# Attention and two MLP layers on one core: the first MLP phase in 256-token tiles, two output blocks to a PSUM bank, and an emission order by due times

## The chip, the core and the metric

One NeuronCore of one Trainium2 chip runs the whole program in one launch. The metric is the device time in microseconds. Engines are named as the profile names them: PE (matmul) and PEld (its weight loads), DVE (vector), ACT (scalar activations), POOL, and SP, which here only issues DMAs.

## What is computed

The reference, cut to what matters (B=4, H=8, S=576, D=64; 2304 tokens of 512 values, d_ff=2048):

```python
scores = q @ k.T / sqrt(64)              # per batch and head, 576 x 576
mask = (rel >= 0) & (rel < 64)           # each query sees itself and the 63 keys before it
attn = exp(scores - rowmax); attn = attn / (rowsum + 1e-9)
x = (attn @ v).transpose(0, 2, 1, 3).reshape(2304, 512)
h = x @ moe_w_in;   x = maximum(0.01 * h, h) @ moe_w_out
h = x @ moe2_w_in;  out = (h * cos(h)) @ moe2_w_out
```

## The kernel before

**Attention** runs in 18 *steps* of 128 tokens, all 8 heads at once, as two halves (the even and the odd heads, `hd` 0 and 1). A step is a chain over four engines. PE makes the scores `qk` into two PSUM buffers (`a_scores`). DVE scales and masks them into `S` and takes the row maxima, half by half (`a_mask`). ACT exponentiates with the row sums (`a_exp`, four instructions a half). DVE inverts the sums (`a_recip`), POOL scales the rows (`a_norm`, L309), PE transposes (`pt`, L317), ACT copies the transposed block to SBUF (`PT`), PE multiplies by the values (`pv`, L329), ACT writes the rounded result `XH` and DVE the remainder `XL`. So `XH` + `XL` hold the layer's input in two parts, step by step.

**The MLPs** multiply in split precision: every product is three matmuls (high by high, high by low, low by high). Each layer's 16 blocks of 128 hidden units are taken in four *phases* of G=4 blocks, so there are eight phases in all. Within a phase the tokens go in tiles, and one tile with one block is a *unit*. A unit `i` has 12 matmuls `h` (L421 to L423: input by w_in, four chunks of the model dimension), then on ACT and DVE the activation `ca`, its rounded part `gh` and its remainder `gl` (L431, L436), then 12 matmuls `y` (L505, called `o` below: `emit_O`), which add into four output accumulators over the four units of a tile. After a tile's last unit ACT copies the four accumulators to `YFa` or `YFb` (`evac`). The first phase's tiles hold 256, 256, 512, 512, 512 and 256 tokens, so it has units 0 to 23, and unit 24 begins the second phase.

**The weights** arrive as 64-bit words and are rebuilt on the core, one matrix block (a *weight unit* `u`) at a time: ACT takes the words apart (`wa`, `wf`), DVE sets the bits (L200, L201, L205), POOL multiplies and adds (`wf`, L210; `wa`, L214), ACT rounds to `wh`, POOL makes the remainder `wl` (L226). The first phase needs eight weight units; those of the second need SBUF that attention gives back when its last step is over (`a_close`), so only three of them can be begun before that.

**The order of the work.** From the start to the end of the first phase, and two units further, a greedy planner written in Python (`ListSchedule`) sets the order in which instructions are emitted, with a table of assumed durations and of buffers. Each engine then runs its own instructions strictly in that order. The planner takes, of all the steps that could go next, the one with the earliest start plus a fixed `bias` by kind. Buffers are counted in it: `S` 4, `PT` 2, PSUM banks `y` 4, `h` 2 and `a` 2 (the last for scores, transposes and `pv`). From unit 26 on, a plain loop emits H of unit `i`, its activation, and O of unit `i-2`.

The line that picks the engine for a step that could go to several:

```python
rank = t + us + (DVE_SPARED if engine == "dve" and len(ways) > 1 else 0.0)
```

Of the kernel before, what the change touches and what calls it, by code (L numbers as in the profile page):

```python
# [31 lines left out]
TILES_FIRST = (256, 256, 512, 512, 512, 256)  # L32
# [3 lines left out]
B_MLP = 0.0  # L36
B_W = 0.25
B_W2 = 1.0
B_ATT = 0.0
DVE_SPARED = 2.0  # L40
# [3 lines left out]
class ListSchedule:  # L44
# [11 lines left out]
    def add(self, name, ways, after=(), take=(), give=(), bias=0.0):  # L56
        assert name not in self.ops
        self.ops[name] = (ways, tuple(after), tuple(take), tuple(give), bias)

    def ready(self, name):  # L60
        ways, after, take, give, bias = self.ops[name]
# [11 lines left out]
        for engine, us, fn in ways:  # L73
            t = max(bufs, self.free.get(engine, 0.0))
            for a in after:
                t0, e0 = self.done[a]
                t = max(t, t0 + (0.02 if e0 == engine else 0.35 if e0 == "pe" else 0.2))
            rank = t + us + (DVE_SPARED if engine == "dve" and len(ways) > 1 else 0.0)
            if best is None or rank < best[4]:
                best = (t, engine, us, fn, rank)  # L80
        return best

    def run(self):
        waiting = list(self.ops)
        while waiting:
            best = None
            for name in waiting:
                r = self.ready(name)
                if r is not None and (best is None or r[0] + self.ops[name][4] < best[0]):
                    best = (r[0] + self.ops[name][4], name, r)  # L90
            assert best is not None, waiting[:40]
            _, name, (t, engine, us, fn, _) = best
# [13 lines left out]
def attention_two_mlps(ctx, tc, q, k, v, w_in1, w_out1, w_in2, w_out2, out, seq):  # L106
# [18 lines left out]
    ps_y = ctx.enter_context(tc.tile_pool(name="ps_y", bufs=4, space=bass.MemoryType.PSUM))  # L125
# [216 lines left out]
    def a_close():  # L342
# [4 lines left out]
        late["ps_y2"] = ctx.enter_context(tc.tile_pool(name="ps_y2", bufs=2, space=bass.MemoryType.PSUM))  # L347
# [130 lines left out]
    def emit_O(i, chunks=None):  # L478
# [4 lines left out]
        first, last = w["first"], w["last"]  # L483
# [4 lines left out]
        for d in range(nacc) if chunks is None else chunks:  # L488
            if first:
                pool = ps_y  # L490
                if "ps_y2" in late:
                    pool = late["ps_y2"] if ycount[0] % 6 >= 4 else ps_y
                    ycount[0] += 1
                ys.append(pool.tile([P, 512], F32, tag="y", name=f"y{i}_{d}"))
            if l == 0:
                y = ys[d][:, :n]
                prods = [(wh[:, 1, d, :], gh[:, :n]), (wh[:, 1, d, :], gl[:, :n]), (wl[:, 1, d, :], gh[:, :n])]
            else:
                y = ys[d]
# [4 lines left out]
            for x, (a, b) in enumerate(prods):  # L504
                mm(y, a, b, start=first and x == 0, stop=last and x == 2)  # L505
            if last:
                e_todo.append((w, d, y))
        if d == nacc - 1:
# [34 lines left out]
    for kind, m in enumerate(masks):  # L543
# [18 lines left out]
        dict(a=2, y=4, h=2, S=4, PT=2, ca=2, g=2, wa=3, wf=2, we=1),  # L562
# [7 lines left out]

    def add_w_dma(x):
# [4 lines left out]
            bias=B_W if x < 2 * G else B_W2,  # L576
# [183 lines left out]
```

## Time and profile before

| | |
|---|---|
| median of 3 runs | 931.75 us (928.1 to 936.08) |
| the profiled execution | 934.54 us, its span 932.7 us |
| mean granted PE clock | 0.977 |
| PE busy | 883.8 us (95%), 5136 matmuls |
| DVE, ACT, POOL busy | 589.1 us (63%), 485.9 us (52%), 306.6 us (33%) |
| DMA | 60.11 MB, mean 64 GB/s, 231 GB/s in the first 23 us |

The profile shows one execution. Its span runs from the first to the last instruction, and the execution's own time is 1.84 us above it. Times in its rows are microseconds from the span's start. In a timeline row stand the start, the duration, the engine and line, what is written and read, and how often; in brackets the idle time before it and what ended it. A matmul's duration is a model that overlaps the next one's, so how fast PE goes is read from the starts.

### The profile page before, as it was taken

The page shows a single profiled execution, that of the slowest core. Times are in us where ns is not written, and L with a number is a line of the kernel's source. Part 1 is how long each engine was busy: PE and PEld are TensorE (multiplying, and loading weights), DVE is VectorE, ACT ScalarE, POOL GpSimd, SP SyncE. Part 2 cuts the span into 40 slices and gives each one's busy share as a digit, 9 for nine tenths or more (in the row PEclk, how much of TensorE's full clock was granted, in tenths as well). Part 3 has the DMA queues.
Part 4 walks back from the last instruction along what each step waited for, and adds up shares of the span by engine and source line. Part 5 has one row for each costly group of instructions (what it writes and reads, how often), then busy time and mean ns, then how long its engine had stood idle before and what let it go on. Part 6 is the DMA issues. An engine that isn't in the chain of part 4 may idle for free.

```text
span 932.7 us, 13579 instructions
## 1 busy us (share of the span) xinstructions
PE 883.8 (95%) x5136; PEld 737.5 (79%) x5136; DVE 589.1 (63%) x935; ACT 485.9 (52%) x1079; POOL 306.6 (33%) x267
## 2 busy tenths in 40 slices
PE   5778979799899999999999999999999999999998
PEld 4667767579688888888888888888887888788886
DVE  5787635355665545555576577776787777876555
ACT  5667555555533333332445467667556556554443
POOL 4772311114733213322367443332332233320000
PEclk9889899899999999999999999999999999999999
DMA  7644433301212101110111111110111011001111
GB/s 231 197 151 147 147 103 109 116 4 46 91 47 67 40 29 46 46 46 23 45 46 50 42 45 46 46 46 22 50 64 41 28 45 46 24 1 46 46 45 69
DMA packets 29089, 60.11 MB, mean 64 GB/s; under 512 B 2464, under 2 KB 11680, under 8 KB 29024
## 3 DMA queue, kind: packets, MB, share of 16 engines
q1 hardware_dynamic: 29024, 59.25, 19.3%
q8 instruction: 40, 0.66, 0.3%
q14 instruction: 25, 0.20, 0.1%
HBM read 54.53 MB, written 4.72 MB: 64 GB/s over the span
## 4 chain that ended last, share of the span: by engine, by line
PE 85%; DVE 7%; ACT 4%; issue 2%; POOL 2%; DMA 1%; SPq 0%; DVEq 0%; ACTq 0%; POOLq 0%
PE y L505 38%; PE h L421 14%; PE h L422 13%; PE h L423 13%; PE pv L329 3%; PE qk L279 2%; PE pt L317 2%; DVE wa L201 1%; POOL S L309 1%; ACT S L297 1%; ACT PT L153 1%; DVE wa L200 1%; DVE we L205 1%; DVE S L287 1%; DVE sm L292 1%
## 5 line engine op out<-in xcount | busy, mean ns | idle before, releaser
L421 PE MATMUL h<-XH,wh 128*128 128x512 f32 (+1 forms) x656 | 243.2, 371 | 6.0 <-DVE ca L443 3.2
L422 PE MATMUL h<-XL,wh 128*128 128x512 f32 (+1 forms) x656 | 240.8, 367 | 0.0
L423 PE MATMUL h<-XH,wl 128*128 128x512 f32 (+1 forms) x656 | 240.6, 367 | 0.1
L226 POOL TENSOR_TENSOR wl<-wa,wh 128x512 fp32r<-128x512 f32 x64 | 85.8, 1343 | 217.6 <-ACT wh L153 216.2
L421 PEld LDWEIGHTS h<-XH,wh 128*128 128x128 f32 x656 | 125.7, 192 | 30.2 <-DVE ca L443 4.5
L436 DVE TENSOR_TENSOR gl<-ca,gh 128x512 fp32r<-128x512 f32 (+1 forms) x164 | 139.2, 848 | 10.3 <-ACT gh L153 10.3
L423 PEld LDWEIGHTS h<-XH,wl 128*128 128x128 f32 x656 | 125.3, 191 | 20.5 <-POOL wl L226 0.3
L422 PEld LDWEIGHTS h<-XL,wh 128*128 128x128 f32 x656 | 125.7, 192 | 19.9
L431 DVE TENSOR_TENSOR ca<-h,ca 128x512 f32<-128x512 f32 (+1 forms) x84 | 51.5, 613 | 132.5 <-ACT ca L153 132.3
L153 ACT ACTIVATE gh<-ca 128x512 fp32r<-128x512 f32 (+1 forms) x164 | 94.4, 576 | 78.0 <-PE y L505 60.2
L210 POOL TENSOR_TENSOR wf<-wf,we 128x512 bf16<-128x512 bf16 x63 | 73.3, 1163 | 179.2 <-DVE we L205 169.7
L505 PE MATMUL y<-gh,wh 128*128 128x512 f32 (+1 forms) x336 | 123.9, 369 | 0.0
L505 PE MATMUL y<-gh,wl 128*128 128x512 f32 (+1 forms) x336 | 121.5, 362 | 1.8 <-POOL wl L226 1.8
L505 PE MATMUL y<-gl,wh 128*128 128x512 f32 (+1 forms) x336 | 121.4, 361 | 0.5 <-DVE gl L436 0.5
L505 PE MATMUL y<-wh,gh 128*128 128x512 f32 x288 | 112.4, 390 | 0.3 <-ACT gh L153 0.3
L505 PE MATMUL y<-wl,gh 128*128 128x512 f32 x288 | 112.2, 390 | 0.0
L505 PE MATMUL y<-wh,gl 128*128 128x512 f32 x288 | 112.2, 389 | 0.0
L461 DVE SCALAR_TENSOR_TENSOR cb<-ca,h 128x512 f32<-128x512 int32 (+1 forms) x80 | 50.7, 633 | 84.2 <-ACT ca L459 84.2
L153 ACT ACTIVATE ca<-h 128x512 f32<-128x512 f32 (+1 forms) x83 | 44.6, 538 | 112.8 <-PE h L423 106.4
L468 ACT ACTIVATE cb<-ca 128x512 f32<-128x512 f32 (+1 forms) x80 | 47.2, 590 | 79.5 <-DVE ca L462 79.5
L459 ACT ACTIVATE ca<-h 128x512 int32<-128x512 f32 (+1 forms) x80 | 44.2, 552 | 80.0 <-PE h L423 78.9
L214 POOL TENSOR_TENSOR wa<-wa,wf 128x512 f32<-128x512 f32 x63 | 79.4, 1260 | 4.7
(59 smaller groups left out, 1265.1 us busy)
## 6 DMA issues: line engine op xcount, KB each, us to landing
st<-in_moe_w_in_dram SPq DMA_DIRECT2D x32, 512.0 KB, 3.4
st<-in_moe_w_out_dram SPq DMA_DIRECT2D x32, 512.0 KB, 3.4
v<-in_v_dram SPq DMA_DIRECT2D x35, 256.0 KB, 2.9
kT<-in_k_dram SPq DMA_DIRECT2D x17, 384.0 KB, 3.8
qT<-in_q_dram SPq DMA_DIRECT2D x18, 256.0 KB, 3.9
out_dram<-YFa SPq DMA_DIRECT2D x12, 256.0 KB, 2.2
out_dram<-YFb SPq DMA_DIRECT2D x6, 256.0 KB, 2.1
kT<-in_k_dram SPq DMA_DIRECT2D x1, 256.0 KB, 3.3
```

Of the source, the lines that this page charges most:

```text
L153: nc.scalar.activation(out=out_, in_=in_, func=AF.Copy, scale=scale)
L210: engines[engine].tensor_tensor(out=f, in0=f, in1=e, op=ALU.mult)
L214: engines[engine].tensor_tensor(out=a, in0=a, in1=f, op=ALU.add)
L226: engines[engine].tensor_tensor(out=wl, in0=mid.pop(u)[0], in1=wh.bitcast(F32), op=ALU.subtract)
L421: mm(h[:, :n], wh[:, 0, kk, :], xh, start=kk == 0, stop=False)
L422: mm(h[:, :n], wh[:, 0, kk, :], xl, start=False, stop=False)
L423: mm(h[:, :n], wl[:, 0, kk, :], xh, start=False, stop=kk == KD - 1)
L431: nc.vector.tensor_tensor(out=ca[i], in0=hps.pop(i)[:, :work[i]["n"]], in1=ca[i], op=ALU.max)
L436: nc.vector.tensor_tensor(out=gl[:, :n], in0=ca.pop(i), in1=gh[:, :n].bitcast(F32), op=ALU.subtract)
L461: nc.vector.scalar_tensor_tensor(out=b, in0=kk, scalar=-PI2_A, in1=h, op0=ALU.mult, op1=ALU.add)
L468: nc.scalar.activation(out=b, in_=a, func=AF.Sin, scale=0.5)
L505: mm(y, a, b, start=first and x == 0, stop=last and x == 2)
```

## The change

It has three parts, all in the planned stretch (the plain loop behind it is the same but for which pool a PSUM bank comes from).

First, the first phase goes in nine tiles of 256 tokens, so it has units 0 to 35, and unit 36 begins the second phase. Its accumulators are *packed*: two output blocks of 256 columns share one PSUM bank, so a tile takes two banks where it took four, and one copy takes two blocks out.

Second, the buffers are dealt out anew: `y` 2 banks, `a` 4 banks, `S` 6, `PT` 3. Only step 0 uses the `y` banks for its scores (`LEAD`, before: steps 0 and 1).

Third, the planner picks differently. Of all steps that could start within 0.05 us of the earliest, it takes the one with the earliest *due* time: tile `t` is due at 18 `t`, attention step `i` at 9 `i` - 30, the first eight weight units from -22 on, the next at 30 and every 8 us after. The assumed durations are new, and DVE may take POOL's part of the first eight weight units at a smaller handicap (0.3 in place of 2.0).

```diff
-TILES_FIRST = (256, 256, 512, 512, 512, 256)
+TILES_FIRST = (256,) * 9
...
-DVE_SPARED = 2.0
+SAME = dict(pe=0.0, dve=0.12, act=0.12, pool=0.05, dma=0.0, none=0.0)
+AT_ONCE = 0.05
+TILE_US, STEP_AHEAD = 18.0, 30.0
+W_AHEAD, LATE_FROM, LATE_US = 22.0, 30.0, 8.0
+SPARED_FIRST, SPARED = 0.3, 2.0
...
-            rank = t + us + (DVE_SPARED if engine == "dve" and len(ways) > 1 else 0.0)
+            rank = t + us + (spared if engine == "dve" and len(ways) > 1 else 0.0)
...
-                if r is not None and (best is None or r[0] + self.ops[name][4] < best[0]):
-                    best = (r[0] + self.ops[name][4], name, r)
+            now = min(r[0] for _, r in ready) + AT_ONCE
+            name, (t, engine, us, fn, _) = min(
+                (x for x in ready if x[1][0] <= now), key=lambda x: (self.ops[x[0]][4], x[1][0])
+            )
...
-    ps_y = ctx.enter_context(tc.tile_pool(name="ps_y", bufs=4, space=bass.MemoryType.PSUM))
+    ps_y = ctx.enter_context(tc.tile_pool(name="ps_y", bufs=2, space=bass.MemoryType.PSUM))
-    sp = act_es.enter_context(tc.tile_pool(name="sp", bufs=4))
-    ptp = act_es.enter_context(tc.tile_pool(name="ptp", bufs=2))
+    sp = act_es.enter_context(tc.tile_pool(name="sp", bufs=6))
+    ptp = act_es.enter_context(tc.tile_pool(name="ptp", bufs=3))
-    ps_a = act_es.enter_context(tc.tile_pool(name="ps_a", bufs=2, space=bass.MemoryType.PSUM))
+    ps_a = act_es.enter_context(tc.tile_pool(name="ps_a", bufs=4, space=bass.MemoryType.PSUM))
...
+            if packed:
+                y = ys[d // 2][:, d % 2 * n:(d % 2 + 1) * n]
...
+                mm(y, a, b, start=first and x == 0 and not (packed and d % 2), stop=last and x == 2,
+                   skip_group_check=packed)
-            if last:
+            if last and not packed:
                 e_todo.append((w, d, y))
+            elif last and d % 2:
+                e_todo.append((w, d - 1, ys[d // 2]))
...
-        op("wm", ways(lambda e: w_mult(u, e), pool=1.11, dve=0.36), [f"wb{u}"], [], [("we", f"wb{u}")])
+        op("wm", ways(lambda e: w_mult(u, e), pool=1.24, dve=0.42), [f"wb{u}"], [], [("we", f"wb{u}")])
...
+    def s_due(i):
+        return TILE_US / 2 * i - STEP_AHEAD
...
-    LEAD = TILES_FIRST[0] // P
+    LEAD = 1
```

The order on each engine moves with this. Two places follow; the figure behind a name's letters is the step, the unit or the weight unit, and a trailing figure only numbers the buffer.

On DVE, before, around the first unit's activation `ca0` (the bits of weight units 4 and 6 stand beside it, steps 2 and 3 are the scores):

```order
L200 TENSOR_SCALAR wa4_360<-wa4_360 128x512
L201 SCALAR_TENSOR_TENSOR wa4_360<-st4_324,wa4_360 128x512
L205 TENSOR_SCALAR we4_387<-wa4_360 128x512
L287 SCALAR_TENSOR_TENSOR S2_0_365<-qk2_0_364,m2_112 128x512
L292 TENSOR_REDUCE sm2_401<-S2_0_365 128x4
L287 SCALAR_TENSOR_TENSOR S2_1_367<-qk2_1_366,m2_112 128x512
L292 TENSOR_REDUCE sm2_401<-S2_1_367 128x4
L431 TENSOR_TENSOR ca0_420<-h0_395,ca0_420 128x256
L157 TENSOR_SCALAR wf6_458<-st6_362 128x512
L200 TENSOR_SCALAR wa6_409<-wa6_409 128x512
L201 SCALAR_TENSOR_TENSOR wa6_409<-st6_362,wa6_409 128x512
L205 TENSOR_SCALAR we6_460<-wa6_409 128x512
```

On DVE, with the change, around the same `ca0` (`wf5`, `wa5`, `wf7` and `wa7` written from themselves are the product and the sum that POOL made before; their line numbers are one less than before's):

```order
L209 TENSOR_TENSOR wf5_492<-wf5_492,we5_525 128x512
L213 TENSOR_TENSOR wa5_456<-wa5_456,wf5_492 128x512
L199 TENSOR_SCALAR wa7_546<-wa7_546 128x512
L200 SCALAR_TENSOR_TENSOR wa7_546<-st7_497,wa7_546 128x512
L204 TENSOR_SCALAR we7_582<-wa7_546 128x512
L337 TENSOR_TENSOR XL_80<-pv2_553,XH_79 128x4x128
L209 TENSOR_TENSOR wf7_575<-wf7_575,we7_582 128x512
L430 TENSOR_TENSOR ca0_573<-h0_516,ca0_573 128x256
L213 TENSOR_TENSOR wa7_546<-wa7_546,wf7_575 128x512
L435 TENSOR_TENSOR gl0_640<-ca0_573,gh0_639 128x256
L430 TENSOR_TENSOR ca1_612<-h1_536,ca1_612 128x256
L286 SCALAR_TENSOR_TENSOR S4_0_591<-qk4_0_590,m1_111 128x512
```

Before, `ca0` stands behind the bits of three weight units; with the change it stands behind the bits of all eight, and behind eleven products, sums and remainders of them that were POOL's, and `gl0`, on which the first `y` matmul waits, stands just behind it.

On PE, before, where step 10's transposes stand (the rows ahead of them are the end of the scores of step 11 and unit 11's second half of `y`):

```order
L279 MATMUL qk11_0_1540<-kT11_1308,qT11_1310 64x128
L279 MATMUL qk11_1_1542<-kT11_1308,qT11_1310 64x128
L505 MATMUL y8_2_1385<-gh11_1507,wh3_557 128x512
L505 MATMUL y8_2_1385<-gl11_1508,wh3_557 128x512
L505 MATMUL y8_2_1385<-gh11_1507,wl3_558 128x512
L505 MATMUL y8_3_1420<-gh11_1507,wh3_557 128x512
L505 MATMUL y8_3_1420<-gl11_1508,wh3_557 128x512
L505 MATMUL y8_3_1420<-gh11_1507,wl3_558 128x512
L317 MATMUL pt10_0_1589<-ident_109,S10_0_1484 128x128 x4
L317 MATMUL pt10_1_1599<-ident_109,S10_1_1486 128x128 x4
L329 MATMUL pv10_1611<-PT10_0_1604,v10_1417 64x64
```

On PE, with the change, at the same transposes (step 10's scores end 74 rows ahead of this piece, step 11's 57):

```order
L420 MATMUL h15_1649<-XH_79,wh3_439 128x256
L421 MATMUL h15_1649<-XL_80,wh3_439 128x256
L422 MATMUL h15_1649<-XH_79,wl3_440 128x256
L316 MATMUL pt10_0_1663<-ident_109,S10_0_1491 128x128 x4
L420 MATMUL h15_1649<-XH_79,wh3_439 128x256
L421 MATMUL h15_1649<-XL_80,wh3_439 128x256
L422 MATMUL h15_1649<-XH_79,wl3_440 128x256
L420 MATMUL h15_1649<-XH_79,wh3_439 128x256
L421 MATMUL h15_1649<-XL_80,wh3_439 128x256
L422 MATMUL h15_1649<-XH_79,wl3_440 128x256
L316 MATMUL pt10_1_1680<-ident_109,S10_1_1493 128x128 x4
L420 MATMUL h16_1685<-XH_79,wh0_293 128x256
```

Before, both transposes of step 10 and its `pv` stand back to back behind the tile's last `y`; now `h` matmuls of the next units stand ahead of each transpose, and `pv10` follows 28 rows further on.

More of the change, by code (lines that the diff above doesn't have):

```diff
@@ L54, in __init__, with add @@
         self.given = {p: {} for p in pools}
-    def add(self, name, ways, after=(), take=(), give=(), bias=0.0):
+    def add(self, name, ways, after=(), take=(), give=(), due=0.0, spared=0.0):
         assert name not in self.ops
-        self.ops[name] = (ways, tuple(after), tuple(take), tuple(give), bias)
+        self.ops[name] = (ways, tuple(after), tuple(take), tuple(give), due, spared)
     def ready(self, name):
-        ways, after, take, give, bias = self.ops[name]
+        ways, after, take, give, due, spared = self.ops[name]
         bufs = 0.0
@@ L85, in run @@
         while waiting:
-            best = None
-            for name in waiting:
-                r = self.ready(name)
-                if r is not None and (best is None or r[0] + self.ops[name][4] < best[0]):
-                    best = (r[0] + self.ops[name][4], name, r)
-            assert best is not None, waiting[:40]
-            _, name, (t, engine, us, fn, _) = best
+            ready = [(name, r) for name in waiting if (r := self.ready(name)) is not None]
+            assert ready, waiting[:40]
+            now = min(r[0] for _, r in ready) + AT_ONCE
+            name, (t, engine, us, fn, _) = min(
+                (x for x in ready if x[1][0] <= now), key=lambda x: (self.ops[x[0]][4], x[1][0])
+            )
             waiting.remove(name)
@@ L346, in a_close @@
         late["tb"] = ctx.enter_context(tc.tile_pool(name="tb", bufs=2))
[L347 removed]
+        late["ps_y2"] = ctx.enter_context(tc.tile_pool(name="ps_y2", bufs=4, space=bass.MemoryType.PSUM))
         YF[1] = late["yb"].tile([P, (T - T_SPLIT) // P, KD, P], F32, name="YFb")
@@ L482, in emit_O @@
         gh, gl = g_hl[i]
-        first, last = w["first"], w["last"]
+        first, last, packed = w["first"], w["last"], w["packed"]
         nacc = KD if l == 0 else n // P
@@ L488, in emit_O @@
         for d in range(nacc) if chunks is None else chunks:
-            if first:
+            if first and not (packed and d % 2):
                 pool = ps_y
-                if "ps_y2" in late:
-                    pool = late["ps_y2"] if ycount[0] % 6 >= 4 else ps_y
+                if not packed:
+                    pool = ps_y if ycount[0] % 6 < 2 else late["ps_y2"]
                     ycount[0] += 1
                 ys.append(pool.tile([P, 512], F32, tag="y", name=f"y{i}_{d}"))
+            if packed:
+                y = ys[d // 2][:, d % 2 * n:(d % 2 + 1) * n]
+            else:
+                y = ys[d][:, :n] if l == 0 else ys[d]
             if l == 0:
-                y = ys[d][:, :n]
                 prods = [(wh[:, 1, d, :], gh[:, :n]), (wh[:, 1, d, :], gl[:, :n]), (wl[:, 1, d, :], gh[:, :n])]
             else:
-                y = ys[d]
                 sl = slice(d * P, (d + 1) * P)
@@ L665, in add_unit @@
             ls.add(
-                f"o{i}_{d}", ways(lambda e, d=d: emit_O(i, [d]), pe=0.648 * f), after,
-                ["y"] if w["first"] else [], [("g", f"gh{i}")] if d == KD - 1 else [], bias=B_MLP,
+                f"o{i}_{d}", ways(lambda e, d=d: emit_O(i, [d]), pe=0.04 + 0.64 * f), after,
+                ["y"] if w["first"] and d % 2 == 0 else [], [("g", f"gh{i}")] if d == KD - 1 else [], due=u_due(i),
             )
-            if w["last"]:
+            if w["last"] and d % 2:
                 after = [f"o{i}_{d}"]
-                if d:
-                    after.append(f"ev{i}_{d - 1}")
+                if d > 1:
+                    after.append(f"ev{i}_{d - 2}")
                 elif i >= G:
```

72 lines of the change are left out of this document (38 added, 34 removed).

## Prediction

> **What bounds the kernel now.** I read the page first: PE is busy in nearly every slice, and the slices where it is not lie at the left.
>
> ```profile
> PE   5778979799899999999999999999999999999998
> ```
>
> So I cut the span at events of the program. PE's timeline gives them: the first `h`, the first `y` of unit 0, the first `h` of the second phase (unit 24, the first of 512 columns behind 256).
>
> ```profile
> 26.87 0.58 PE L421 MATMUL h<-XH,wh 128*128 128x256 f32 x1
> ...
> 52.63 0.28 PE L505 MATMUL y<-gh,wh 128*128 128x256 f32 x1
> 52.75 0.28 PE L505 MATMUL y<-gl,wh 128*128 128x256 f32 x1
> ...
> 225.26 0.40 PE L421 MATMUL h<-XH,wh 128*128 128x512 f32 x1
> ```
>
> The table by stages (the cuts between are the first `h` of the tiles of 512):
>
> ```profile
> core 0: us, PE busy (x) PEld busy (x) DVE busy (x) ACT busy (x) POOL busy (x), PEclk, DMA share, GB/s
> ...
> 26.90:52.60 25.70, 19.41 (x207) 16.69 (x205) 19.54 (x32) 17.75 (x55) 16.91 (x15) 0.87 0.54 170
> 52.60:97.00 44.40, 35.69 (x423) 31.61 (x421) 32.26 (x57) 29.68 (x101) 22.60 (x19) 0.87 0.47 159
> 97.00:141.60 44.60, 39.15 (x387) 30.48 (x384) 22.64 (x39) 26.09 (x88) 10.92 (x10) 0.94 0.38 123
> 141.60:187.20 45.60, 40.55 (x388) 31.49 (x385) 21.18 (x36) 25.97 (x88) 8.60 (x8) 0.89 0.35 108
> 187.20:225.30 38.10, 38.10 (x284) 32.29 (x282) 18.75 (x33) 21.11 (x61) 10.86 (x9) 0.95 0.05 15
> 225.30:256.50 31.20, 26.72 (x123) 21.69 (x122) 19.60 (x26) 17.60 (x34) 21.10 (x16) 0.95 0.26 85
> ```
>
> Between 52.6 and 225.3 no engine is full: DVE and ACT run at 50 to 75%, and a busy PE is not PE at its peak. How much of these 172.6 us PE needs comes from starts of its rows:
>
> ```profile
> 102.12 1.10 PE L279 MATMUL qk<-kT,qT 64*64 64x128 f32 x32
> 103.15 0.50 PE L421 MATMUL h<-XH,wh 128*128 128x512 f32 x1
> ...
> 107.41 0.60 PE L317 MATMUL pt<-ident,S 128*128 128x128 f32 x4
> 107.76 0.47 PE L505 MATMUL y<-gh,wh 128*128 128x512 f32 x1
> ...
> 116.78 1.08 PE pv L329 x32
> ...
> 253.87 2.74 PE y L505 x12
> ```
>
> A matmul of 512 columns takes 2.74/12 = 0.228 us, one of 256 takes 52.75 - 52.63 = 0.12. A step's scores take 1.03 to 1.10 (I use 1.10), a half's transposes 0.35, with the changeover 0.4, the values 1.08. PE's order before has, from the first `y` to unit 24, 204 matmuls of 256 columns (24.5 us), 288 of 512 (65.7), 13 score groups (14.3), 28 halves of transposes (11.2) and 14 of values (15.1): 130.8 us. So 41.8 us are lost here. The waits name 19.2 of them for this stretch, of which these rows are 14.3:
>
> ```profile
> PE pt L317 <- POOL S L309: 10.6, 9, 3.7
> PE pv L329 <- ACT PT L153: 3.7, 7, 1.1
> ```
>
> Most of the rest is the granted clock: 0.13, 0.06, 0.11 and 0.05 of the four stages from 52.6 on are 5.8 + 2.7 + 5.0 + 1.9 = 15.4 us. **The bound of the first phase is thus the attention chain where PE has too little beside it**, and the half clock that follows such waits.
>
> **The change part by part. Length of the chain, and what lies beside it.** Three steps show how long the chain is from the end of the scores to the first transpose, where PE waited for it:
>
> ```profile
> 26.09 0.86 PE L279 MATMUL qk<-kT,qT 64*64 64x128 f32 x10
> ...
> 38.41 2.29 PE L317 MATMUL pt<-ident,S 128*128 128x128 f32 x8 [4.86 <-POOL S L309]
> ...
> 50.07 1.10 PE L279 MATMUL qk<-kT,qT 64*64 64x128 f32 x30 [1.09 <-DVE XL L338]
> ...
> 60.62 0.55 PE L317 MATMUL pt<-ident,S 128*128 128x128 f32 x3 [3.73 <-POOL S L309]
> ...
> 120.09 1.10 PE L279 MATMUL qk<-kT,qT 64*64 64x128 f32 x32
> ...
> 129.64 0.66 PE L317 MATMUL pt<-ident,S 128*128 128x128 f32 x4 [1.51 <-POOL S L309]
> ```
>
> 38.41 - 26.95 = 11.5 us (step 2, among the weights), 60.62 - 51.17 = 9.45 (step 4), 129.64 - 121.19 = 8.45 (step 10, in the quiet middle). Beside it, PE's order before holds 3.25 to 9.3 us of other work (steps 11 and 15: 3.25; 10 and 14: 6.6). The new order, counted with the same prices, holds for steps 4 to 17: 10.5, 10.9, 8.4, 12.1, 9.1, 9.0, 8.0, 14.9, 8.7, 9.0, 8.4, 9.9, 7.2, 7.3 us. What a chain lacks of cover is PE's wait. With a chain of 8.45 these steps lack 2.9 us in all, with 9.45 they lack 9.8, with 11.5 they lack 32. ACT and DVE have the same work per token as before and less time for it (26.09 us of ACT for 512 tokens in the third row of the table), so their queues are fuller than in the quiet middle; I take 9.45, and 5 us for values, remainders and `gl` (values alone 3.7 before, in the waits): **15 us lost, ends 5 and 37**. The lower end leaves 2 of those 5 us; the upper is 32 and 5. I charge no half clock on top: all covers but a few exceed the wait, so PE should not stand long. If it still falls as before, up to 15 us come back; that is in the upper half of the range.
>
> **PE's work.** With the change, from unit 0's first `y` to unit 36, which begins the second phase, PE has 807 matmuls of 256 columns (96.8 us), 13 score groups (14.3), 28 halves of transposes (11.2) and 15 of values (16.2): 138.5 us. It is more than 130.8 since 27 matmuls of `h` and step 3's values less have gone before the first `y`, and since two matmuls of 256 take 0.240 us where one of 512 takes 0.228: 288 times 0.012 are 3.5 us of cost, which this sum holds.
>
> **The start.** The first `y` needs `gl0` and all of DVE's work ahead of it. The same view by shapes, DVE from 0 to 225 us:
>
> ```profile
> L292 DVE TENSOR_REDUCE sm<-S 128x4 f32<-128x512 f32 x36 | 24.7, 686 | 1.2
> L287 DVE SCALAR_TENSOR_TENSOR S<-qk,m 128x512 f32<-128x512 f32 x36 | 24.4, 678 | 22.2 <-PE qk L279 22.2
> ...
> L436 DVE TENSOR_TENSOR gl<-ca,gh 128x512 fp32r<-128x512 f32 x12 | 12.3, 1025 | 4.4 <-ACT gh L153 4.4
> L201 DVE SCALAR_TENSOR_TENSOR wa<-st,wa 128x512 uint32<-128x512 uint32 x12 | 10.7, 891 | 0.4
> ...
> L200 DVE TENSOR_SCALAR wa<-wa 128x512 uint32<-128x512 uint32 x12 | 7.0, 586 | 2.1 <-ACT wa L153 2.0
> L205 DVE TENSOR_SCALAR we<-wa 128x512 uint16<-128x512 uint16 x12 | 6.8, 562 | 1.0
> ...
> L214 DVE TENSOR_TENSOR wa<-wa,wf 128x512 f32<-128x512 f32 x1 | 1.4, 1432 | 0.0
> ...
> L210 DVE TENSOR_TENSOR wf<-wf,we 128x512 bf16<-128x512 bf16 x1 | 0.4, 374 | 0.0
> ```
>
> Up to `gl0` stand eight masks and eight maxima (10.9 us), the bits of eight weight units (8 x (0.586 + 0.891 + 0.562) = 16.3), six products that were POOL's (2.2) and four sums (5.7), two remainders `wl`, which DVE did not make before (as L436: 2.1), and 18 small ones, by estimate 0.43 each on the mean (7.8; ten are reciprocals with their addition, shorter than any row here, a few as long as L292): 45 us. DVE begins at 7.39:
>
> ```profile
> 7.39 0.69 DVE L287 SCALAR_TENSOR_TENSOR S<-qk,m 128x512 f32<-128x512 f32 x1 [5.73 <-PE qk L279]
> ```
>
> That is 52.4 if it never waits, and neighbours overlap a little; I take **the first `y` at 55, ends 49 and 62**, against 52.63. The first `h` will be late too (it needs `XL` of step 1, which now stands behind the bits of six weight units), but it hides behind DVE. So do the loads. SP's order changes, too: the weights now stand between the steps' loads, and up to weight unit 7 it asks for 10 MB.
>
> ```profile
> GB/s 231 197 151 147 147 103 109 116 4 46 91 47 67 40 29 46 46 46 23 45 46 50 42 45 46 46 46 22 50 64 41 28 45 46 24 1 46 46 45 69
> ```
>
> At the rates of the first two slices (23.3 us each: 5.4 and 4.6 MB) they are there at 46.6 us, ahead of DVE's last bits. Without that cover the first `y` moves with them, and ACT, whose copies of the words stand in order between the exponentials, holds the attention up until they land.
>
> **The border of the phases.** The rest of the weights still wait for the last step. Step 17's values end at 208.98, 16.3 us ahead of unit 24:
>
> ```profile
> 207.83 1.15 PE L329 MATMUL pv<-PT,v 128*64 128x64 f32 x32
> ```
>
> The new order has 132 matmuls there, 15.8 us, and again only weight units 8, 10 and 12 prepared: so the 4.5 us that PE is idle after 225.3 stay. If POOL's chain were later, they grow by as much; the small difference of 0.5 is all I see. Packing itself costs no PE time, halves the number of accumulator copies, and `YFb` still waits for the end of attention. From there on the program is as before.
>
> **Sum.** Unit 36 begins at 55 + 138.5 + 15 = 208.5, against 225.3: 16.8 us less. The profiled execution (934.54) would take 917.7; the median before is 2.8 lower, so **915 us**.
>
> **A rule against it.** DVE's L201 takes 0.69 us at 18.34 and 1.53 at 21.19, where POOL's sum is under way:
>
> ```profile
> 18.34 0.69 DVE L201 SCALAR_TENSOR_TENSOR wa<-st,wa 128x512 uint32<-128x512 uint32 x1
> ...
> 21.19 1.53 DVE L201 SCALAR_TENSOR_TENSOR wa<-st,wa 128x512 uint32<-128x512 uint32 x1
> ...
> 20.87 1.30 POOL L214 TENSOR_TENSOR wa<-wa,wf 128x512 f32<-128x512 f32 x1
> ```
>
> POOL ends at 22.17, and DVE 0.55 later, as if it had stood still until then. The Trainium skill ("SBUF — State Buffer", section "SBUF: two separate sides") calls the port pair that both use an exclusive lock, which blocks the loser for a whole instruction when DVE reads two SBUF inputs. The trace agrees. By that rule the twelve operations moved to DVE are of the kind that meets the lock; that is the first rival. The one such sum that DVE made before took 1.432 us.
>
> **The rivals.** *The start gives the gain back.* If each of the twelve moved operations meets POOL once, at 1.53 - 0.69 = 0.84 us, DVE ends 10 us later: first `y` at 65, gain 6.8, **925 us**. For it: DVE is the fullest engine of the first stage (19.54 of 25.7 us). Against: POOL has twelve operations fewer there. *The chain stretches (slower).* One mechanism: ACT and DVE serve attention, units and weights in strict order, and with a tile every 17 us each chain queues as in step 2. At 11.5 us the waits are 37; with the first `y` at 60, unit 36 begins at 235.5: **942 us**. It decides from a loss of 31.8 us on (225.3 - 55 - 138.5), that is from a chain of about 10.7. For it: the two early chains; against: 8.45 in the middle, and more buffers, so that scores need not wait. *Nothing waits:* lost 5, first `y` at 50, 36 begins at 193.5: **900 us**. That the steps do not move ahead at all can be left out: the order shows `pt10` spread among `h`.
>
> **How the numbers follow.** Forecast (905 to 921) 0.60, start 0.20, slower 0.12, nothing waits 0.08. The range runs from the last case, 900, to 932 (first `y` at 60, 27 lost: nothing gained); it leaves out the slower case and thin tails on both sides, less than 2 in 10. About 1% is what a measurement of this kernel can tell from no change, so faster means below 922.4: the forecast, the last case and a little off for the forecast's upper tail, 0.66; the start rival and that tail 0.23 within; 0.11 above 941.
>
> **What would show it.** The first `y` near 55 on PE's timeline; `pt` waits for POOL of at most 10 us from there, in pieces of about 1 us; a clock near 1.0 from 60 to 200; the first 512-column `h` near 208; the stage behind it as long as before. Wrong it would be if DVE is not full before 50 (then DMA or ACT's order holds the start), or if `y` waits for its bank: two accumulator banks leave 1.2 us between units 15 and 16, where ACT's copy stands behind four exponentials.

## The result, and the profile after

The changed kernel takes **906.08 us** (median of 4 runs, 905.41 to 906.57) beside 933.69 us of the kernel before in the same comparison: ratio 0.971, 95% interval 0.966 to 0.976. The profiled execution took 906.46 us with a span of 904.7, 28.0 less than before. The kernel before varies more from run to run (over all comparisons 925.96 to 937.52 us, with mean granted clocks from 0.990 down to 0.971), and its profiled execution, 934.54 us, is one of the longer ones.

The busy slices of the page, after: the dips in the sixth, eighth and eleventh slice are gone, and the start is emptier.

```profile
PE   4489999999999999999999999999999999999998
```

PE's timeline after, at the same three events (first `h`, first `y`, first `h` of the second phase, now unit 36):

```profile
41.32 0.56 PE L420 MATMUL h<-XH,wh 128*128 128x256 f32 x1
...
55.30 0.41 PE L507 MATMUL y<-gh,wh 128*128 128x256 f32 x1
...
201.55 0.40 PE L420 MATMUL h<-XH,wh 128*128 128x512 f32 x1
```

The table by stages, after, and PE's waits from the first `y` to unit 36:

```profile
core 0: us, PE busy (x) PEld busy (x) DVE busy (x) ACT busy (x) POOL busy (x), PEclk, DMA share, GB/s
0.00:41.30 41.30, 18.41 (x216) 14.54 (x217) 33.59 (x53) 24.62 (x79) 23.99 (x36) 0.80 0.68 233
41.30:55.30 14.00, 10.55 (x107) 9.54 (x106) 13.69 (x23) 9.59 (x24) 5.96 (x5) 0.74 0.56 186
55.30:87.00 31.70, 31.34 (x433) 29.11 (x433) 27.42 (x51) 26.17 (x99) 16.44 (x15) 0.99 0.56 184
87.00:131.00 44.00, 44.00 (x573) 42.21 (x572) 24.51 (x52) 32.60 (x116) 10.37 (x10) 1.00 0.38 122
131.00:183.80 52.80, 52.80 (x684) 50.03 (x682) 30.63 (x62) 36.38 (x127) 10.19 (x10) 1.00 0.28 89
183.80:201.50 17.70, 16.58 (x134) 15.97 (x133) 12.66 (x18) 12.65 (x27) 10.45 (x9) 1.00 0.16 60
201.50:232.00 30.50, 29.24 (x138) 23.86 (x138) 18.62 (x25) 15.40 (x28) 18.44 (x15) 1.00 0.26 86
```

```profile
PE y L507 <- DVE gl L435: 1.1, 2, 0.5
PE pv L328 <- ACT PT L152: 0.3, 1, 0.3
```

From 55.3 to 201.5 PE waits 1.4 us by name where it waited 19.2 before, `pt` never waits for POOL, and the clock is at 0.99 to 1.00. The stretch is 146.25 us long and holds 138.5 of work by the prediction's prices, so 7.75 are lost. Step 10 shows why `pt` no longer waits. PE and POOL after:

```profile
107.91 1.98 PE L278 MATMUL qk<-kT,qT 64*64 64x128 f32 x64
...
117.08 0.60 PE L316 MATMUL pt<-ident,S 128*128 128x128 f32 x4
```

```profile
115.66 2.04 POOL L308 TENSOR_TENSOR S<-S,sm 128x512 f32<-128x512 f32 x2 [5.67 <-DVE sm L304]
```

The scores of steps 10 and 11 go in one piece (64 matmuls in four banks). The first of the two normalizations ends near 116.7 (115.66 + 1.04), and the transposes follow at 117.08 with no idle time in brackets: PE came to them just after the data.

To compare kernels, one measure serves for all that follows. **Lost** is time on PE's way to the second phase less the work there, which is counted from each kernel's order with the prediction's prices (151.0 us in the kernel before, 154.4 in the changed one). It is split at the first `y`; the tail runs from the second phase to the end of the span. All ratios are to the kernel before, run on the same chip.

| kernel | median us | ratio [95%] | banks for attention | first `y` | lost ahead of it | lost behind it | tail |
|---|---|---|---|---|---|---|---|
| before | 931.75 | 1 | 2 | 52.6 | 32.4 | 41.8 | 707.5 |
| changed | 906.08 | 0.971 [0.966, 0.976] | 4 | 55.3 | 39.4 | 7.75 | 703.1 |
| e1 old rule | 901.42 | 0.969 [0.966, 0.973] | 4 | 81.3 | 35.0 | 10.7 | 699.5 |
| e10 old SBUF buffers | 904.74 | 0.970 [0.965, 0.975] | 4 | 48.1 | 32.3 | 12.7 | 703.3 |
| e3 charge 2.0 | 905.15 | 0.973 [0.970, 0.977] | 4 | 49.4 | 29.5 | 15.9 | 703.2 |
| e14 other table | 901.47 | 0.969 [0.964, 0.974] | 4 | 45.7 | 27.3 | 16.2 | 702.5 |
| e15 other table | 906.72 | 0.975 [0.970, 0.980] | 4 | 46.0 | 29.8 | 19.7 | 701.1 |
| e11 lead of 60 | 910.92 | 0.976 [0.971, 0.982] | 4 | 64.5 | 40.0 | 14.2 | 700.9 |
| e6 longer chain | 918.44 | 0.987 [0.982, 0.992] | 4 | 56.4 | 40.5 | 18.7 | 703.3 |
| e2 all old buffers | 926.44 | 0.994 [0.992, 0.997] | 2 | 52.1 | 37.3 | 28.1 | 703.2 |
| e9 two banks | 930.28 | 0.999 [0.995, 1.002] | 2 | 49.9 | 36.3 | 35.1 | 703.5 |
| e13 old rule, two banks | 928.73 | 0.996 [0.993, 1.000] | 2 | 50.7 | 31.6 | 34.0 | 707.5 |
| e4 due times alone | 938.24 | 1.007 [1.003, 1.011] | 2 | 49.3 | 33.1 | 49.1 | 703.5 |

So the 28.0 us of the span divide into: first `y` 2.7 later, work behind it 7.7 more, loss behind it 34.1 less, tail 4.3 less.

### The profile page after: what moved, and what is told of

It reads as the page before. It is cut to its first block, busy times and chain, and to the rows that moved or that the text cites. A ratio compares the mean times of both kernels' runs of the same rounds, so it can differ in the third digit from the quotient of the medians.

```text
span 904.7 us, 14203 instructions
## 1 busy us (share of the span) xinstructions
PE 868.3 (96%) x5424; PEld 743.5 (82%) x5424; DVE 599.8 (66%) x963; ACT 488.7 (54%) x1101; POOL 294.7 (33%) x257
## 4 chain that ended last, share of the span: by engine, by line
PE 86%; DVE 8%; ACT 2%; issue 2%; DMA 1%; SPq 0%; POOL 0%; ACTq 0%; DVEq 0%; POOLq 0%
PE y L507 40%; PE h L420 14%; PE h L421 14%; PE h L422 14%; PE pv L328 2%; DVE wa L200 1%; PE pt L316 1%; DVE wa L199 1%; PE qk L278 1%; DMA qT<-in_q_dram 1%; DVE S L286 1%; DVE we L204 1%; DMA st<-in_moe_w_in_dram 1%; DVE YFa L535 1%; DVE sm L291 0%
## 5 line engine op out<-in xcount | busy, mean ns | idle before, releaser
L420 PE MATMUL h<-XH,wh 128*128 128x512 f32 (+1 forms) x704 | 250.9, 356 | 3.2 <-DVE ca L442 3.2
L420 PEld LDWEIGHTS h<-XH,wh 128*128 128x128 f32 x704 | 134.0, 190 | 24.3 <-DVE ca L442 4.6
L421 PEld LDWEIGHTS h<-XL,wh 128*128 128x128 f32 x704 | 134.1, 190 | 18.9 <-DVE XL L337 1.2
L422 PEld LDWEIGHTS h<-XH,wl 128*128 128x128 f32 x704 | 134.0, 190 | 17.6
L430 DVE TENSOR_TENSOR ca<-h,ca 128x256 f32<-128x256 f32 (+1 forms) x96 | 53.2, 554 | 131.2 <-ACT ca L152 131.0
L507 PE MATMUL y<-gh,wh 128*128 128x256 f32 (+1 forms) x384 | 131.2, 342 | 0.7 <-ACT gh L152 0.7
L507 PE MATMUL y<-gl,wh 128*128 128x256 f32 (+1 forms) x384 | 129.8, 338 | 1.7 <-DVE gl L435 1.6
L507 PE MATMUL y<-gh,wl 128*128 128x256 f32 (+1 forms) x384 | 129.0, 336 | 0.0
L152 ACT ACTIVATE ca<-h 128x256 f32<-128x256 f32 (+1 forms) x96 | 46.7, 488 | 112.7 <-PE h L422 103.7
L507 PEld LDWEIGHTS y<-gl,wh 128*128 128x128 f32 x384 | 72.8, 190 | 10.5 <-DVE gl L435 3.0
```

The costliest lines, as they stand in the source:

```text
L152: nc.scalar.activation(out=out_, in_=in_, func=AF.Copy, scale=scale)
L420: mm(h[:, :n], wh[:, 0, kk, :], xh, start=kk == 0, stop=False)
L421: mm(h[:, :n], wh[:, 0, kk, :], xl, start=False, stop=False)
L422: mm(h[:, :n], wl[:, 0, kk, :], xh, start=False, stop=kk == KD - 1)
L430: nc.vector.tensor_tensor(out=ca[i], in0=hps.pop(i)[:, :work[i]["n"]], in1=ca[i], op=ALU.max)
L507: mm(y, a, b, start=first and x == 0 and not (packed and d % 2), stop=last and x == 2, skip_group_check=packed)
```

## The experiments

### Which part of the change does it

**e1, the old rule of choice** with the new tiles, packing, buffers and durations:

```diff
-            now = min(r[0] for _, r in ready) + AT_ONCE
-            name, (t, engine, us, fn, _) = min(
-                (x for x in ready if x[1][0] <= now), key=lambda x: (self.ops[x[0]][4], x[1][0])
-            )
+            name, (t, engine, us, fn, _) = min(ready, key=lambda x: x[1][0] + self.ops[x[0]][4])
...
```

(All due times are set to 0, those of the weights to 0.25 and 1.0.)

> The changed kernel with the old rule of choice (earliest start, weights set back by 0.25 and 1.0 us, no due times); tiles, packing, buffers and durations stay new. Theory (the due times make the gain, since they put 8 to 12 us of other PE work between a step's scores and its transposes): in this order the covers of steps 4 to 17 are 4.1 to 8.8 us, and against a chain of 9.0 us they lack 29 us in all (6 in the changed kernel, 33 in the kernel before); so waits of pt for POOL come back, 10 to 20 us of them, and the half clock behind them; 925 to 940 us. Rival (tiles and buffers alone make the gain): within 6 us of 906, waits of pt under 3 us.

Measured 901.42 us (901.01 to 902.86): **the theory missed**, and the rival had the time, though not its "waits of pt under 3 us". PE's slices on the page and PE's waits behind the first `y`, e1:

```profile
PE   5788799999999999999999999999999999999998
```

```profile
PE pt L313 <- POOL S L305: 3.1, 3, 2.3
PE pt L313 <- DVE sm L288: 1.6, 1, 1.6
```

Without due times, attention goes first as fast as its engines let it: the last `pv` ends at 114.8 (183.8 in the changed kernel), the first `y` comes at 81.3, and from 115 us on PE has nothing but `h` and `y`. The short covers stand mostly ahead of the first `y`, where PE is not full anyway: 35.0 us are lost there against 39.4. The second phase begins at 201.55, just as in the changed kernel, and 12 more `y` matmuls (1.4 us) are done by then. **Due times are not what makes the first phase shorter.** With four banks the new rule is even 4.7 us slower than the old one (906.08 and 901.42, in different comparisons); between the profiled executions it is 3.6 us, all of it in the tail.

**e9 and e10, the buffers split.** e9 has two banks for attention, e10 the old `S` and `PT`:

```diff
 e9:
-    ps_a = act_es.enter_context(tc.tile_pool(name="ps_a", bufs=4, ...
+    ps_a = act_es.enter_context(tc.tile_pool(name="ps_a", bufs=2, ...
 e10:
-    sp = act_es.enter_context(tc.tile_pool(name="sp", bufs=6))
-    ptp = act_es.enter_context(tc.tile_pool(name="ptp", bufs=3))
+    sp = act_es.enter_context(tc.tile_pool(name="sp", bufs=4))
+    ptp = act_es.enter_context(tc.tile_pool(name="ptp", bufs=2))
```

(The planner's table of buffers is changed with them.)

> The changed kernel with two banks for attention in place of four (in the planner too); six score buffers, three transposed ones, tiles, packing and due times stay. Theory (of the buffers it is the banks that count: a step's scores take two, so the next step's scores can't be issued ahead of this step's transposes): the covers of steps 4 to 17 lack 38.6 us against a chain of 9.0 (6.0 in the changed kernel, 33.4 with all old buffers, where 28 us were lost), so about 30 us are lost from the first y on; second phase at 222 to 226, 924 to 932 us. Rival (score buffers count): 906 to 912 us.

> The other half of that split: four banks, but the four score buffers and two transposed ones of the kernel before. Theory (banks count): the covers lack 10.3 us, so 8 to 12 are lost where the changed kernel loses 7.75; 905 to 911 us. Rival (score buffers count): 920 us or more.

e9 took 930.28 us, e10 904.74; second phases at 225.9 and 199.4. Both times came as the theory had them, within a microsecond; the losses behind the first `y` were above it (35.1 for about 30, 12.7 for 8 to 12). PE's waits behind the first `y`, e9, and a piece of its timeline:

```profile
PE pv L328 <- ACT PT L152: 8.8, 13, 1.0
PE pt L316 <- POOL S L308: 2.9, 4, 1.5
```

```profile
103.74 0.66 PE L316 MATMUL pt<-ident,S 128*128 128x128 f32 x4
105.36 0.33 PE L328 MATMUL pv<-PT,v 128*64 128x64 f32 x2 [0.96 <-ACT PT L152]
106.15 1.15 PE L328 MATMUL pv<-PT,v 128*64 128x64 f32 x30 [0.46 <-ACT PT L152]
107.23 0.66 PE L316 MATMUL pt<-ident,S 128*128 128x128 f32 x4
```

Transposes, values and the next step's transposes stand back to back, since each of them needs one of the two banks that the scores need as well. **The two banks that packing sets free are 24 us of the change's 28**, and the score buffers in SBUF nothing (0.970 beside 0.971).

**e2, all old buffers of attention** under the new rule:

```diff
-        dict(a=4, y=2, h=2, S=6, PT=3, ca=2, g=2, wa=3, wf=2, we=1),
+        dict(a=2, y=2, h=2, S=4, PT=2, ca=2, g=2, wa=3, wf=2, we=1),
...
```

(The three pools are changed with the planner's table.)

> The changed kernel with the old buffers of attention (2 banks, 4 score buffers, 2 transposed ones, also in the planner); tiles, packing and due times stay new. Theory: the buffers are what lets a step's scores run ahead; with the old ones the covers fall to 5.5 to 6.9 us at every step (lack 33 us against a chain of 9.0, as much as before), so about 19 us of waits and some of the 15 us of half clock come back: 925 to 940 us. Rival (due times alone do it, the buffers are only room): within 6 us of 906.

Measured 926.44 us, as the theory had it; but its mean clock behind the first `y` is 1.00, so that the 28.1 us lost hold no half clock: 14.8 are waits by name, and the rest is taken up with e6.

**e13, old rule and two banks**, which completes the square with e1:

```diff
 e1, and:
-    ps_a = act_es.enter_context(tc.tile_pool(name="ps_a", bufs=4, ...
+    ps_a = act_es.enter_context(tc.tile_pool(name="ps_a", bufs=2, ...
```

> The run with the old rule of choice, now with two banks for attention in place of four; small tiles, packing, six score buffers stay. Theory (the banks make the gain under either rule): the covers lack 40.9 us against a chain of 9.0, as many as with due times and two banks (38.6, where 36 us were lost from the first y on); first y 50 to 55, 135.3 us of work behind it, 30 to 36 lost, second phase at 217 to 226, 920 to 930 us. Rival (the old rule finds a good order with two banks as well): 901 to 910 us.

Measured 928.73 us, second phase at 220.0, 34.0 us lost behind the first `y`: as the theory had it. Its waits behind the first `y` and those of the next 31 us:

```profile
PE pt L313 <- POOL S L305: 9.8, 9, 4.1
```

```profile
PE h L417 <- DVE ca L427: 3.4, 1, 3.4
```

The first line is the old picture, in small tiles. From two to four banks the old rule gains 27 us, the new one 24; and e13, which has the small tiles, the packing, six `S` buffers and the new durations but two banks, stands at 0.996 of the kernel before. The second line is the border: e13's tail is 707.5 like before's, while every run with the changed kernel's due times for tiles and attention has 703.1 to 703.5, e4's large tiles included; and the last `pv` ends 17.9 us ahead of the second phase in e13, 17.7 in the changed kernel. **The 4.3 us of the tail are the due times' doing** where attention ends this late; e1 reaches 699.5 without them, its last `pv` being 86.7 us ahead. The due times put the late weights earlier: POOL's first product of a late unit starts 11.7 us behind the last `pv` in e13, 13.8 in the kernel before (222.75 against 208.98), 8.1 in the changed kernel (191.90 against 183.81). POOL before, then PE and POOL with the change:

```profile
222.75 1.16 POOL L210 TENSOR_TENSOR wf<-wf,we 128x512 bf16<-128x512 bf16 x1 [4.19 <-ACT ca L153]
```

```profile
182.66 1.15 PE L328 MATMUL pv<-PT,v 128*64 128x64 f32 x32
```

```profile
191.90 1.21 POOL L209 TENSOR_TENSOR wf<-wf,we 128x512 bf16<-128x512 bf16 x1 [1.61 <-DVE we L204]
```

**e4, due times alone** on the old tiles and buffers:

```diff
-TILES_FIRST = (256,) * 9
+TILES_FIRST = (256, 256, 512, 512, 512, 256)
-    ps_y = ... bufs=2   ps_a = ... bufs=4   sp = ... bufs=6   ptp = ... bufs=3
+    ps_y = ... bufs=4   ps_a = ... bufs=2   sp = ... bufs=4   ptp = ... bufs=2
...
```

(Packing is off, and steps 0 and 1 use the `y` banks, as before.)

> The kernel before (tiles of 512, one block to a bank, old buffers) with the due times and new durations alone. Theory (due times need small tiles and buffers): scores of two steps of four now stand only 1.1 to 1.9 us ahead of their transposes; the covers lack 57 us against a chain of 9.0 (33 before), so waits of pt rise from 10.6 to 20 us or more: 935 to 960 us. Rival (due times alone make the gain): 905 to 915 us.

Measured 938.24 us, slower than before, with 49.1 us lost behind the first `y` (57 us of covers lacking); waits of `pt` for POOL are 9.6 us, fewer than the 20 expected, and 5.3 of `qk` for `S` came in their place. The size of it was met, the form in part.

### The room in the chain, and the clock

**e6, a longer chain** in the changed kernel's own order:

```diff
+        if i >= 2:
+            nc.gpsimd.tensor_tensor(out=st, in0=st, in1=ones.unsqueeze(2).to_broadcast([P, NPR, P]), op=ALU.mult)
...
```

> The changed kernel, same order, with one more operation of POOL behind each normalization from step 2 on (a product with ones, in place; the output is unchanged): the first half's chain grows by 1.04 us, the second half's by 2.08. Theory (the four banks leave room, but the covers are only just longer than the chains: transposes start 0.2 to 2.0 us behind the end of their normalization): by the room of each step 11.5 us of waits appear, fewer where one wait makes room for the next; 6 to 12 us slower than the changed kernel, 911 to 918 us. Rival (the chain is wholly off the path): within 2 us of 906.

Measured 918.44 us, 12.4 more, just above the theory's range; second phase at 213.60. PE's waits, and the stretch from the first `y`, e6:

```profile
PE pt L319 <- POOL S L313: 8.6, 15, 1.1
PE y L510 <- DVE gl L438: 1.1, 2, 0.6
```

```profile
56.42:213.60 157.18, 147.37 (x1816) 137.40 (x1816) 98.07 (x182) 109.10 (x366) 78.11 (x72) 1.00 0.34 108
```

One microsecond more in each half and fifteen waits are back: the changed kernel has little room left in the chain. The loss grew by 10.9 us, the waits by name by 8.3; the other 2.6 stand as busy time (147.37 against 144.77 in the changed kernel), about 0.17 for each wait. **In this order a wait on PE cost more than its name says.** What the other kernels lose beyond their waits is not this alone: the changed kernel, with three waits of 1.4 us in all, has 6.3 us of it (7.75 less 1.4), the kernel before 7.2 (41.8 less 19.2 of waits and 15.4 of half clock, over 22 waits), e2 13.3 (28.1 less 14.8, over 27 waits). So some 6 us seem to be work that the prices put too low, and what e2 has above that stays open.

**e8, the kernel before with its long waits filled** by matmuls whose results are overwritten:

```diff
+        for _ in range({4: 28, 6: 10, 10: 11, 14: 11}.get(i, 0) if hd == 0 else 0):
+            nc.tensor.matmul(ps[:, 0:2, :], XH[:, 0, 0:P], XH[:, 0, 0:2 * P], start=True, stop=True)
```

> The kernel before, with extra matmuls of 256 columns (28 at step 4, 10 at 6, 11 at 10 and at 14; their results are overwritten) put on PE ahead of the first half's transposes, where PE waits 3.7 and three times 1.5 us for POOL. The output is unchanged. Theory (the half clock of the first phase, 15.4 us, follows from these waits): the clock from 52.6 to the second phase goes from 0.91 to 0.97 or more, and 8 to 12 us are gained: 920 to 925 us. Rival (the clock falls for another reason, or the gain of the change is in the waits alone): clock within 0.02 of 0.91, 930 to 936 us.

Measured 928.72 us (924.84 to 930.65) beside 934.89, ratio 0.994 (0.991 to 0.998); clock from the first `y` to the second phase 0.96, and that stretch 5.4 us shorter (167.27). So it lies between the two. The same four windows before, and with the waits filled (the column behind POOL is the clock):

```profile
60.00:68.00 8.00, 6.85 (x54) 6.12 (x55) 7.09 (x9) 4.80 (x16) 7.57 (x7) 0.58 0.18 73
92.00:100.00 8.00, 7.20 (x72) 5.77 (x69) 3.94 (x8) 2.79 (x10) 2.31 (x2) 0.58 0.53 176
128.00:148.00 20.00, 14.55 (x167) 11.19 (x167) 7.51 (x16) 11.28 (x42) 4.07 (x4) 0.91 0.37 120
176.00:192.00 16.00, 13.67 (x117) 10.69 (x118) 4.15 (x7) 4.69 (x15) 2.04 (x2) 0.57 0.22 67
```

```profile
60.00:68.00 8.00, 7.38 (x82) 6.74 (x81) 7.86 (x10) 6.36 (x23) 8.00 (x7) 1.00 0.41 134
92.00:100.00 8.00, 6.95 (x92) 5.46 (x92) 5.42 (x10) 4.47 (x18) 2.67 (x3) 1.00 0.68 217
128.00:148.00 20.00, 16.81 (x160) 12.85 (x160) 5.30 (x10) 8.67 (x30) 2.04 (x2) 0.66 0.29 89
176.00:192.00 16.00, 12.63 (x162) 9.94 (x163) 6.66 (x13) 7.96 (x27) 2.04 (x2) 1.00 0.22 67
```

Three of the four stretches of half clock are gone, and the one at 128 to 148 became longer, though step 10's wait there was filled just as step 14's. One trace on each side can't show that filling the waits did it, since the half clock of the kernel before varies without any change; what stands beside it is the mean clock of all runs of this comparison, 0.983 to 0.994 (median 0.988) with the waits filled and 0.973 to 0.988 (median 0.976) before. So half clock goes with the waits, but which wait sets it off is not told by this run.

### The start, and other tables

**e3, the charge for DVE** at the first eight weight units back at 2.0:

```diff
-SPARED_FIRST, SPARED = 0.3, 2.0
+SPARED_FIRST, SPARED = 2.0, 2.0
```

> The changed kernel with the planner's charge for DVE on the first eight weight units back at 2.0 us, so that their products, sums and remainders are mostly POOL's again; all else new. Theory (DVE's work holds the first y at 55.3, 47.3 us of it from 7.4 on): some 10 us of operations leave DVE, part of it comes back as POOL's chain; first y 48 to 54, PE's work behind it 134.6 and waits as in the changed kernel; 898 to 908 us. Rival (moving them to DVE is what makes the start possible; POOL's slower chain then holds it): first y 58 or later, 908 to 920 us.

Measured 905.15 us, first `y` at 49.4: as the theory had the start. DVE is busy 39.14 us up to there, against 47.28 up to 55.30 in the changed kernel. In the runs with the new tiles the first `y` comes 8.0 to 10.5 us behind the sum of DVE's busy time up to it (e1 81.27 and 70.85, e11 64.45 and 54.28, e10 48.11 and 39.83), but for e13 with 12.8 (50.71 and 37.93); in the kernel before it was 18.9 (52.63 and 33.72). But of the 5.9 us that the first `y` came earlier, the second phase kept 1.6: 15.9 us are lost behind it, `h` waiting 3.4 for `ca` in one piece, with a clock of 0.98.

**e11, a lead of 60 us:**

```diff
-TILE_US, STEP_AHEAD = 18.0, 30.0
+TILE_US, STEP_AHEAD = 18.0, 60.0
```

> The changed kernel with attention due 60 us ahead of its tile in place of 30. Theory: two more steps are pulled into the start, where PE stands idle, and cost DVE about 3.3 us each there (first y 58 to 62); 130 us of work are left behind it and 10 to 13 are lost (the covers lack 13.1); the last step ends 35 us ahead of the second phase in place of 16, so the weights of that phase are ready and its start costs 3.7 us less, as with the old rule; 898 to 903 us. Rival (DVE's longer start and the lower covers take back what the border gives): 905 to 912 us.

Measured 910.92 us: a miss, the rival was right. The tail gave 2.2 us and not 3.7, the first `y` came at 64.5, later than expected, and 14.2 us were lost behind it. More lead under due times puts more attention on DVE at the start, and what the tail gives back does not pay for it.

**e14 and e15, other numbers in the table:**

```diff
 e14:
-TILE_US, STEP_AHEAD = 18.0, 30.0
-W_AHEAD, LATE_FROM, LATE_US = 22.0, 30.0, 8.0
-SPARED_FIRST, SPARED = 0.3, 2.0
+TILE_US, STEP_AHEAD = 16.0, 30.0
+W_AHEAD, LATE_FROM, LATE_US = 16.0, 30.0, 8.0
+SPARED_FIRST, SPARED = 1.0, 1.0
 e15 (with e10's buffers):
+TILE_US, STEP_AHEAD = 17.0, 36.0
+W_AHEAD, LATE_FROM, LATE_US = 30.0, 30.0, 8.0
+SPARED_FIRST, SPARED = 2.0, 1.0
```

> The changed kernel with other numbers in the table: 16 us to a tile, weights due 16 us ahead in place of 22, the charge for DVE 1.0 in place of 0.3 and 2.0. Theory (the start is DVE's sum; what POOL takes back shortens it, and the covers stay): first y 47 to 50, 136 us of work behind it, 7 to 12 lost (the covers lack 5.4 us); second phase at 192 to 198, 896 to 902 us. Rival (an earlier first y is lost again, as where the charge was 2.0: first y 6 us earlier, second phase 1.6): second phase at 199 to 202, 903 to 907 us.

> Four banks with the old four score buffers and two transposed ones, 17 us to a tile, attention due 36 us ahead, weights 30, the charge for DVE 2.0 at the start and 1.0 behind it. Theory: first y 46 to 49, 138.2 us of work behind it, 10 to 14 lost (lack 12.2); the last step ends 20 us ahead of the second phase, which may give 1 us there; 898 to 904 us. Rival, as for the other: 903 to 907 us.

e14 took 901.47 us (901.40 to 902.15), within the theory's range, with the first `y` at 45.7 and the second phase at 197.85; but it lost 16.2 us behind the first `y` where 7 to 12 were expected. e15 took 906.72, its rival's time. PE's waits of e14 show what has come up in place of the chain:

```profile
PE y L507 <- DVE gl L435: 4.7, 6, 1.5
PE h L420 <- DVE ca L430: 1.9, 3, 1.3
```

DVE is fuller there (113.1 us busy of 152.2, 95.2 of 146.25 in the changed kernel): five normalizations and six operations on weights that could be POOL's are DVE's, and with the earlier start the bits of ten weight units fall into the stretch in place of six. PE now waits for DVE. e1 and e14 are the fastest kernels run here, 4.6 us below the changed kernel by medians of runs that do not overlap, though from other comparisons; their ratios' intervals overlap its own, since the kernel before varies more.

## Why the prediction was right, point by point

**Start: right, by terms that cancel.** 55 was said, 55.30 came, with DVE full ahead of it (13.69 of 14.0 us). Its busy time was 47.3 for a sum of 45. DVE's groups up to 55.3, after:

```profile
L200 DVE SCALAR_TENSOR_TENSOR wa<-st,wa 128x512 uint32<-128x512 uint32 x8 | 8.4, 1048 | 0.3
L199 DVE TENSOR_SCALAR wa<-wa 128x512 uint32<-128x512 uint32 x8 | 8.3, 1040 | 0.0
L291 DVE TENSOR_REDUCE sm<-S 128x4 f32<-128x512 f32 x9 | 6.2, 686 | 0.3
L286 DVE SCALAR_TENSOR_TENSOR S<-qk,m 128x512 f32<-128x512 f32 x9 | 6.1, 681 | 5.5 <-PE qk L278 5.5
L213 DVE TENSOR_TENSOR wa<-wa,wf 128x512 f32<-128x512 f32 x4 | 4.3, 1076 | 0.1
L204 DVE TENSOR_SCALAR we<-wa 128x512 uint16<-128x512 uint16 x8 | 4.1, 517 | 0.3
```

The bits took 20.8 us where 16.3 were put, and a ninth mask stood in it; the four sums took 4.3 where 5.7 were put. The cost came through the collisions that the first rival spoke of, but mostly on L199 and L200. The twelve moved operations took 8.4 us where 10.0 were put; two of the four sums met POOL (1.52 and 1.41 us, the other two 0.69 and 0.68), and the price of 1.432 already held that. So the bits cost 4.5 us more than put, and not 10.

**PE's work: too low, it seems.** 138.5 us was put. PE is busy 144.77 of the stretch's 146.25 us and waits 1.4 by name, so some 6 us are neither waiting nor in the sum. Where they lie was not separated.

**Lost behind the first `y`: the mis-sized term**, which is why the second phase began at 201.55 and not near 208. 15 were put (9.8 for chains longer than their covers, 5 for the rest); 7.75 came, and only 1.4 of them are waits. The 9.8 were nothing: `pt` never waited for POOL. The chain was put at 9.45 us throughout; where covers were shortest (steps 16 and 17, counted at 7.2 and 7.3) it took 6.6 and 7.6 us from the end of the scores to the end of the first normalization, and only where covers were long (10.5 us and more) did it take 10.4 and more. Step 17's rows, PE and POOL:

```profile
170.99 1.10 PE L278 MATMUL qk<-kT,qT 64*64 64x128 f32 x32
...
179.91 0.60 PE L316 MATMUL pt<-ident,S 128*128 128x128 f32 x4
```

```profile
178.68 2.04 POOL L308 TENSOR_TENSOR S<-S,sm 128x512 f32<-128x512 f32 x2 [5.97 <-ACT XH L152]
```

The scores end at 172.09 and the first normalization near 179.72, later than the counted cover of 7.3 us would reach; but PE took 7.8 us for that cover, so it came just behind the data. Here two errors cancel: by these numbers a PE as fast as priced would have waited about 0.3 us. What room there was is small, 0.2 to 2.0 us at most steps, as e6 shows. The half clock, left out of the sum, did not come. For the profiled execution 917.7 was worked out and 906.46 came: about 7.2 us of the difference stand in this term, 4.3 at the border.

**What the prediction did not see is why the covers grew.** It spoke of the new order as a whole, and its second rival had "more buffers, so that scores need not wait" only as a word against. e1, e9 and e13 show that the order's rule is not needed and the two banks are. The forecast rested on the covers counted in the order itself, so it did not depend on what made them. Among kernels with two banks that count sets e4 apart (57 us lacking, 49.1 lost) but does not rank the others: before, e2, e9 and e13 lack 33, 33, 39 and 41 and lost 41.8, 28.1, 35.1 and 34.0. It failed for e1, since a cover counts for nothing where PE has no other work.

**Border: wrong by 4.3 us.** "The 4.5 us that PE is idle after 225.3 stay" held only for the count of weight units begun before. Their order behind the last step changed too, and PE is idle 1.3 of the 30.5 us behind 201.5. The row on POOL in "if POOL's chain were later" was the right place to look; it was earlier.

**Rivals.** The start gave nothing back; the chain did not stretch (it decides from 31.8 us of loss, 7.75 came; with the covers as listed and 5 us for the rest that is a chain of about 11.1 us, not 10.7). "Nothing waits" had the loss nearly right (5) and the start wrong (50): 900 was put for it, and 906 lies between it and the forecast.

**The lock.** The rule that was weighed can be read here in rows. DVE's L199 and what POOL does beside it, after:

```profile
25.18 1.26 DVE L199 TENSOR_SCALAR wa<-wa 128x512 uint32<-128x512 uint32 x1
31.46 0.42 DVE L199 TENSOR_SCALAR wa<-wa 128x512 uint32<-128x512 uint32 x1
...
43.67 0.42 DVE L199 TENSOR_SCALAR wa<-wa 128x512 uint32<-128x512 uint32 x1
48.36 1.26 DVE L199 TENSOR_SCALAR wa<-wa 128x512 uint32<-128x512 uint32 x1
```

```profile
23.22 2.93 POOL L308 TENSOR_TENSOR S<-S,sm 128x512 f32<-128x512 f32 x2
...
46.84 2.49 POOL L308 TENSOR_TENSOR S<-S,sm 128x512 f32<-128x512 f32 x2 [0.41 <-DVE sm L304]
```

POOL ends at 26.15 and 49.33, and L199 ends 0.29 us behind it both times; the two of the eight with POOL idle take 0.42, the other six 1.06 to 1.38. The Trainium skill ("SBUF — State Buffer", section "SBUF: two separate sides") says that the exclusive lock is taken by a DVE operation with two SBUF inputs or in a two-port mode. The trace agrees with the blocking; L199 reads one input, and no row here shows which mode it runs in.

## What to carry to other kernels

Where PE waits for a chain over other engines, count the buffers that the chain and PE's next work both need, and the work that the order can put between: here two more PSUM banks were worth 24 to 27 us under either rule of choice, and due times on the old tiles and buffers cost 6. Measure each variant by one number per stage, its length less PE's work in it; it showed at once that an earlier start was lost again behind it. And a wait can cost more than its name: 0.17 us each in e6, and in the kernel before stretches of half clock went with the waits.

## What was not expected of the hardware

Waits and the granted clock go together less simply than was thought. e6 has fifteen waits of `pt` of up to 1.1 us and e2 seven of up to 1.4, both at a mean clock of 1.00 from the first `y` on, while the kernel before has a stretch at 0.57 for 16 us (176 to 192) in which PE is busy 13.67 of them. In e8 such a stretch moved and grew where the wait before it had been filled. What sets it off stays open.
